# A later exponential in an attention pipeline, and a split, earlier load of the local q and k

## The chip, the cores and the metric

The kernel runs on one core of one Trainium2 chip. The metric is the device time of one execution in microseconds (us); of several runs the median is taken. The core has a matrix engine (TensorE, "PE" in the profile, with its weight loads as "PEld"), a vector engine (VectorE, DVE), an activation engine (ScalarE, ACT), a general engine (GpSimd, POOL) and an engine that issues transfers (SyncE, SP); each works through its own instructions in order, and semaphores tie them together. Sixteen DMA engines carry the transfers.

## The reference

Attention over 2 batches, 8 heads, 576 tokens and 64 features, in float32. Heads 0 to 3 see a local band (the 32 last positions), heads 4 to 7 a strided pattern (positions equal modulo 32, not later). The result, as 1152 tokens of 512 features, goes through two feed-forward stages.

```python
scores = scale * np.matmul(q, k.transpose(0, 1, 3, 2))
mask_local = (rel >= 0) & (rel < 32)
mask_strided = (rel >= 0) & (pos[None, :] % 32 == pos[:, None] % 32)
attn = softmax(np.where(masks, scores, -1e9)); x = attn @ v
for e in range(4): out += p[:, e:e+1] * (np.maximum(x @ w1[e], 0) @ w2[e])   # x 512 -> 1024 -> 512
gate = 1 / (1 + np.exp(-(out @ w_gate))); val = out @ w_val                  # 512 -> 1536
result = (gate * val) @ w_out
```

## The kernel before

**Attention as a pipeline written out by hand.** The work is cut into 32 groups, 16 for each batch: first 8 strided ones (kind "s"), then 8 local ones (kind "l"). A group passes six stages: `scores` (TensorE, two groups at once, lines 477 to 495, after a matmul that writes the mask into the PSUM tile `sps`), `exp` (VectorE takes the negated row maxima `nm`, line 503; ScalarE does four or three exponentials with their sums, line 505), `norm` (VectorE adds and inverts the sums, lines 512 and 513; GpSimd multiplies, line 514), `transpose` (TensorE, line 521; VectorE copies to the tile `PT`, line 524), `values` (TensorE, line 542; ScalarE copies, line 546; only where the second head of a pair has come) and `split` (VectorE writes the high part of x and GpSimd the low part, lines 561 to 568). The table `STAGES` says how many steps behind the scores a stage runs. In step i the generator `attention()` issues, in the order of the table, each stage for the group that is that many steps back; then a step may issue two matmuls without use (`keep_warm`, line 167), and the transposes that prepare q and k: `qk_strided` (lines 445 to 451) in steps 10 and 11 for the first pair of strided heads of batch 1 and 17 and 18 for its second, `qk_local` (lines 467 to 475) in steps 4 to 6 for batch 0 and 20 to 22 for batch 1. The tiles `sps`, `P`, `nm`, `sm` and `PT` have four buffers each.

**What runs around it.** `attend()` advances the generator by one step, and after some steps it issues loads on SP's queue: after step 6 the strided q and k of batch 1 (into `x2acc`), after step 8 strided values, after 11 the local q and k of batch 1, after 18 and 19 the token weights, after 20 local values. The first `FIRST_GROUPS` steps run alone; from step 14 on each is followed by one step of weight preparation (`prep_some`: a cast on ScalarE, line 425, or a subtraction on VectorE, line 427, in turn). The other 16 steps are interleaved with the matmuls of the first four units of the first feed-forward stage (0.36 steps for each three matmuls of lines 611 to 613). The rest of the kernel is matmul work of the two feed-forward stages, with the preparation of weights (casts and splits into a high and a low part) beside it.

**The order of the first loads on SP's queue**: strided q and k of batch 0 (8 transfers), strided values `vs` for the first pair, local q and k (`ql`, `kl`: 4 transfers of 288 KB), `vs` for the second pair, local values `vl` (5), token weights `ptok`, two pieces of weights `raw`, the strided q and k of batch 1, a third `raw`.

Of the kernel before, what the change touches and what calls it, by code (L numbers as in the profile page):

```python
# [9 lines left out]
F32 = mybir.dt.float32  # L10
# [19 lines left out]
PB_BUFS = 5  # L30
WARM = 11

STAGES = (("values", 6), ("transpose", 4), ("scores", 0), ("exp", 0), ("norm", 2), ("split", 7))
FIRST_GROUPS = 23
ATT_RATE = 0.36


# [1 line left out]
def attn_moe_glu_kernel(ctx, tc, q, k, v, dp, w1, w2, wg, wv, wo, out):  # L39
    nc = tc.nc  # L40
    B, H, S, D = q.shape
# [12 lines left out]
    hp = ctx.enter_context(tc.tile_pool(name="hp", bufs=2))  # L54
# [32 lines left out]
    def load_strided_v(b, c):  # L87
        h0 = 4 + 2 * c
        t = atp.tile([NU, 2, 8 * D], F32, tag="vs", name="vs", bufs=2)
        nc.sync.dma_start(t, v[b, h0:h0 + 2].rearrange("h (u r) d -> u h (r d)", r=8))  # L90
        qkv["vs", b, c] = t

    def load_local(b):
        for nm, src in (("ql", q), ("kl", k)):
            t = hp.tile([128, 9, 2, D], F32, tag="hh" if nm == "ql" else "hl", name=nm)
            for j in range(2):
                nc.sync.dma_start(  # L97
                    t[:, :, j, :],
                    src[b, 2 * j:2 * j + 2].rearrange("h s d -> (h s) d").rearrange("(c p) d -> p c d", p=128),
                )  # L100
            qkv[nm, b] = t

    def load_vl(b):
        t = atp.tile([128, 4, 6, D], F32, tag="vl", name="vl")
# [66 lines left out]
    def make_constants():  # L171

        diff = const.tile([NU, NU], I32, tag="diff", name="diff")
        msf = const.tile([NU, NU], F32, tag="msf", name="msf")
        nc.gpsimd.iota(diff, pattern=[[-1, NU]], base=4 * NU, channel_multiplier=1)
        nc.vector.tensor_scalar(diff, diff, 3, None, ALU.bitwise_and)
        nc.vector.tensor_scalar(msf, diff, 0.0, MASKED, ALU.is_gt, ALU.mult)
        make_identity(nc, ident)
        nc.gpsimd.tensor_copy(identb, ident)
        nc.gpsimd.affine_select(  # L180
            out=mask_s, in_=msf, pattern=[[-1, NU]],
            compare_op=ALU.is_ge, fill=MASKED, base=0, channel_multiplier=1,
        )
        nc.gpsimd.memset(mask_l, 0.0)
        for i0, i1, lead in ((0, 1, 0), (1, 4, 32)):
            m = mask_l[:, i0:i1, :]
            for sign, base in ((1, lead), (-1, 31 - lead)):
                nc.gpsimd.affine_select(
                    out=m, in_=m, pattern=[[0, i1 - i0], [-sign, 128]], compare_op=ALU.is_ge,
                    fill=MASKED, base=base, channel_multiplier=sign,  # L190
                )
# [267 lines left out]
    def qk_local(b, part):  # L459
        for nm, dst in (("ql", QT), ("kl", KT)):  # L460
            src = qkv[nm, b]
            if part == 0:
                dst["l", b] = atp.tile([128, 9 * 128], F32, tag=nm + "T", name=nm + "T")
            t = dst["l", b]
            ps = gp.tile([128, 512], F32, tag="g", name="qkps")
            for i in range(3):
                nc.tensor.transpose(  # L467
                    ps[:, i * 128:(i + 1) * 128],
                    src[:, 3 * part + i].rearrange("p j d -> p (j d)"), ident,
                )  # L470
            dd = t[:, part * 384:(part + 1) * 384]
            if nm == "ql":
                nc.scalar.activation(dd, ps[:, :384], AF.Copy, scale=SCALE)
            else:
                nc.vector.tensor_copy(dd, ps[:, :384])
# [94 lines left out]
    def attention():  # L570

        gs = []
        for b in range(B):
            gs += [("s", b, c, half, hh) for c in range(2) for hh in range(2) for half in range(2)]
            gs += [("l", b, c, half, hh) for half in range(2) for hh in range(2) for c in range(2)]
        n = len(gs)
        stage = dict(values=group_values, transpose=group_transpose, scores=lambda g: i % 2 or pair_scores(gs[i:i + 2]),
                     exp=group_exp, norm=group_norm, split=group_split)
        qk_strided(0, 0, (0,))
        for i in range(n + STAGES[-1][1]):  # L580
            for name, behind in STAGES:
                if 0 <= i - behind < n:
                    stage[name](gs[i - behind])
            if i == 0:
                qk_strided(0, 0, (1,))
            if i < 5 or i % 2 and i < FIRST_GROUPS:
                keep_warm(2)
            for b in range(B):
                at = i - b * n // B
                if b and at in (-6, -5):  # L590
                    qk_strided(b, 0, (at + 6,))
                if at in (1, 2):
                    qk_strided(b, 1, (at - 1,))
                if at in (4, 5, 6):
                    qk_local(b, at - 4)
            yield i


# [213 lines left out]
    with tc.manual_schedule():  # L812
        acc["x2"] = accp.tile([128, KC, NTOK], F32, tag="acc", name="x2acc")
        load_strided_qk(0, 0)
        load_strided_qk(0, 1)
        warm_up()
        make_constants()
        load_strided_v(0, 0)
        load_local(0)
        load_strided_v(0, 1)  # L820
        load_vl(0)
        nc.sync.dma_start(ptok, dp.rearrange("(t p) e -> p t e", p=128))
        load_raw_to(2)
        for T in range(NT - 1):
            alloc_x(T)

        def attend():

            i = next(att, None)
            if i == 6:  # L830
                load_strided_qk(1, 0)
                load_raw_to(3)
            if i == 8:
                load_strided_v(1, 0)
            if i == 11:
                load_local(1)
            if i == 13:
                load_strided_v(1, 1)
            if i == 18:
                token_weights()  # L840
            if i == 19:
                spread_token_weights()
            if i == 20:
                load_vl(1)
            return i

        att = attention()
        for i in range(FIRST_GROUPS):
            attend()
            if i >= 14:  # L850
                prep_some(0, 1)
        n_none = 0
        halves = x_half()
        for n, u in enumerate(units):
            if u == ("u", EARLY, 0):
                for _ in halves:
                    pass
            if u[0] == "u" and u[1] == NST:
                while u[2] not in x2_done:
                    split_x2(1)  # L860
            if n == N_EARLY:
                while attend() is not None:
                    pass
                at_stack.close()
                tmp["p"] = ctx.enter_context(tc.tile_pool(name="tmp", bufs=2, side="right", reuse_waits="tile"))
                alloc_scales()
                late.append(raw_next[0])
                tmp["g"] = ctx.enter_context(
                    tc.tile_pool(name="gp2", bufs=8 - PSUM_BUFS, space=PSUM, side="right", reuse_waits="tile"))
                tmp["w"] = ctx.enter_context(tc.tile_pool(name="wp2", bufs=W_BUFS_2, side="right", reuse_waits="tile"))  # L870
            while any(i in pieces_of(u) for i in waiting()):
                prep_some(n, 1)
            if u == ("d", NST, 0):
                acc["out"] = accp.tile([128, NTB, DM], F32, tag="acc", name="outacc")
            if n >= N_EARLY:
                load_p_some(n)
                load_p_some(n)
            for y in unit_steps(u):
                if n < N_EARLY and y is None:
                    n_none += ATT_RATE  # L880
                    while n_none >= 1:
                        attend()
                        n_none -= 1
                if y == "evac":
                    if n >= N_EARLY:

                        if gated:
                            split_x2(2)
                            continue
                        if x16_next[0] < 2 or n > units.index(("u", EARLY - 1, x16_next[0] - 1)):  # L890
                            if next(halves, "end") != "end":
                                prep_some(n, 1)
                                continue
                    prep_some(n, 3 if u[1] >= NST else 2)
            if u[0] == "d" and u[1] == NST - 1:
                gated.append(x2_half(u[2]))
# [28 lines left out]
```

## Time and profile before

| | |
|---|---|
| median of 3 runs | 683.96 us (681.36 to 684.11) |
| the profiled execution | 678.96 us, its span 677.2 us |
| TensorE busy in the span | 659.5 us, 97% |
| first matmul of the feed-forward work | 58.44 us into the span |
| TensorE's mean granted clock over the span | 0.992 of full |

The span runs from the first to the last instruction that the profiler saw on the core; the 1.76 us beside it lie outside. A busy TensorE is not one at its peak, since the ends of pipelined matmuls are modelled.

### The profile page before, as it was taken

What the parts mean: (1) busy time and instruction counts of PE and PEld (TensorE: products, weight loads), DVE (VectorE), ACT (ScalarE), POOL (GpSimd) and SP (SyncE); (2) the same over time, 40 slices, a digit from 0 to 9 for tenths busy, and PEclk for the clock granted to TensorE, in tenths of its full rate; (3) what the DMA queues carried; (4) which work ended last, traced back from release to release, by engine and by line L of the source; (5) the groups of instructions that cost most, each with busy time, mean ns of one, the idle gap of its engine ahead of it and who ended that gap; (6) DMA issues with size and microseconds to landing.
All of it is one profiled execution on the core that took longest, in us unless ns stands there. A gap on an engine that the chain in (4) does not pass through costs nothing.

```text
span 677.2 us, 11031 instructions
## 1 busy us (share of the span) xinstructions
PE 659.5 (97%) x4257; PEld 431.3 (64%) x4263; DVE 488.9 (72%) x986; ACT 268.9 (40%) x665; POOL 197.9 (29%) x218
## 2 busy tenths in 40 slices
PE   7879999999899999999999999999999999999998
PEld 4657899999766666666665656556655555555554
DVE  3685675878777787779798989887788998822212
ACT  5676541323334444442334252534354364331120
POOL 3463550000222222222354352522154244231110
PEclk9898999999999999999999999999999999999999
DMA  9953133011321233323222213111012321000002
GB/s 190 219 115 92 64 95 121 0 64 32 104 75 63 72 100 102 75 67 121 63 75 63 71 55 94 34 38 55 31 62 83 106 72 53 1 1 0 32 17 94
DMA packets 38965, 48.59 MB, mean 72 GB/s; under 512 B 18460, under 2 KB 23360, under 8 KB 38912
## 3 DMA queue, kind: packets, MB, share of 16 engines
q1 hardware_dynamic: 38912, 47.89, 24.8%
q8 instruction: 33, 0.54, 0.3%
q14 instruction: 20, 0.16, 0.1%
HBM read 45.50 MB, written 2.38 MB: 71 GB/s over the span
## 4 chain that ended last, share of the span: by engine, by line
PE 87%; DVE 8%; DMA 1%; issue 1%; ACT 1%; SPq 1%; POOL 0%; DVEq 0%; ACTq 0%; POOLq 0%
PE gps L611 27%; PE gps L612 27%; PE gps L613 27%; PE o L542 2%; PE sps L495 1%; PE tps L521 1%; DMA kl<-in_k_dram 1%; DVE x2acc L675 1%; DVE wpk L339 1%; SPq L97 1%; PE qkps L467 1%; DMA x2acc<-in_k_dram 1%; DVE x L290 1%; PE sps L485 1%; DVE magn L372 1%
## 5 line engine op out<-in xcount | busy, mean ns | idle before, releaser
L634 POOL TENSOR_TENSOR hl<-t,hh 128x384 f16<-128x384 f32 x72 | 69.3, 962 | 253.9 <-ACT t L633 249.9
L611 PEld LDWEIGHTS <-w 128*128 128x128 f16 x864 | 84.4, 98 | 56.2 <-issue 0.3
L613 PEld LDWEIGHTS <-w 128*128 128x128 f16 x864 | 84.4, 98 | 56.0
L612 PEld LDWEIGHTS <-w 128*128 128x128 f16 x864 | 84.4, 98 | 55.2
L632 ACT ACTIVATE hh<-gps 128x384 f16<-128x384 f32 x72 | 35.2, 489 | 148.2 <-PE gps L613 148.2
L612 PE MATMUL gps<-hl,w 128*128 128x384 f16 x288 | 94.0, 326 | 0.0
L611 PE MATMUL gps<-x,w 128*128 128x384 f16 x288 | 94.0, 326 | 0.0
L611 PE MATMUL gps<-hh,w 128*128 128x384 f16 x288 | 94.0, 326 | 0.0
L612 PE MATMUL gps<-x2p,w 128*128 128x384 f16 x288 | 94.0, 326 | 0.0
L612 PE MATMUL gps<-x,w 128*128 128x384 f16 x288 | 94.0, 326 | 0.0
L613 PE MATMUL gps<-hh,w 128*128 128x384 f16 x288 | 94.0, 326 | 0.0
L613 PE MATMUL gps<-x2p,w 128*128 128x384 f16 x288 | 94.0, 326 | 0.0
L613 PE MATMUL gps<-x,w 128*128 128x384 f16 x288 | 94.0, 326 | 0.0
L611 PE MATMUL gps<-x2p,w 128*128 128x384 f16 x288 | 94.0, 326 | 0.0
L698 POOL TENSOR_TENSOR hl<-gv,hh 128x384 f16<-128x384 f32 x36 | 34.7, 965 | 146.4 <-ACT hh L697 146.4
L355 DVE SCALAR_TENSOR_TENSOR w<-raw,up,w 128x512 f16<-128x512 f32 x48 | 38.3, 799 | 20.3 <-ACT w L353 20.3
L675 DVE TENSOR_TENSOR x2acc<-x2acc,t 128x384 f32<-128x384 f32 x84 | 49.6, 591 | 2.9
L672 DVE SCALAR_TENSOR_TENSOR t<-gps,comb,pb 128x384 f32<-128x384 f32 x72 | 43.8, 609 | 9.9 <-PE gps L613 9.9
L697 ACT CAST hh<-gv 128x384 f16<-128x384 f32 x36 | 18.4, 511 | 81.0 <-DVE gv L696 81.0
L696 DVE SCALAR_TENSOR_TENSOR gv<-gps,sg 128x384 f32<-128x384 f32 x36 | 19.9, 554 | 40.3 <-PE gps L613 40.3
L407 POOL TENSOR_TENSOR w<-magn,w 128x512 f16<-128x512 f32 x36 | 46.1, 1287 | 8.5 <-ACT magn L406 8.1
L505 ACT ACTIVATE P<-sps,nm 72x72 f32<-72x72 f32 (+1 forms) x112 | 36.3, 331 | 28.8 <-DVE sm L512 22.8
(130 smaller groups left out, 1236.2 us busy)
## 6 DMA issues: line engine op xcount, KB each, us to landing
raw<-in_moe_w_dram SPq DMA_DIRECT2D x32, 512.0 KB
raw<-in_moe_w_gate_dram SPq DMA_DIRECT2D x12, 512.0 KB
raw<-in_moe_w_val_dram SPq DMA_DIRECT2D x12, 512.0 KB
raw<-in_moe_w_out_dram SPq DMA_DIRECT2D x12, 512.0 KB
pb<-pd SPq DMA_DIRECT2D x11, 192.0 KB
out_dram<-outacc SPq DMA_DIRECT2D x8, 256.0 KB
vl<-in_v_dram SPq DMA_DIRECT2D x8, 160.0 KB
vs<-in_v_dram SPq DMA_DIRECT2D x4, 288.0 KB
```

The source lines that it names most:

```text
L355: nc.vector.scalar_tensor_tensor(wl[i][:, c, :], part, sc, wh[i][:, c, :], ALU.mult, ALU.subtract)
L407: nc.gpsimd.tensor_tensor(wl[i][:, c, :], f, wh[i][:, c, :], ALU.subtract)
L505: nc.scalar.activation(pp[:, j, :], pv_[:, j, :], AF.Exp, bias=nm[:n, j:j + 1], accum_out=sm[:n, j:j + 1])
L611: nc.tensor.matmul(ps, ah, bh, start=i == 0, stop=False)
L612: nc.tensor.matmul(ps, ah, bl, start=False, stop=False)
L613: nc.tensor.matmul(ps, al, bh, start=False, stop=i == n - 1)
L632: nc.scalar.activation(dh, ps, AF.Relu, scale=DOWN)
L634: nc.gpsimd.tensor_tensor(dl, t, dh, ALU.subtract)
L672: nc.vector.scalar_tensor_tensor(t, ps, cc, pb[e, T], ALU.mult, ALU.mult)
L675: nc.vector.tensor_tensor(a, a, t, ALU.add)
L696: nc.vector.scalar_tensor_tensor(gv, pv_, DOWN, sg, ALU.mult, ALU.mult)
L698: nc.gpsimd.tensor_tensor(dl, gv, dh, ALU.subtract)
```

## The change

The stages `exp` and all behind it run one step later against the scores, and the steps that run alone are 24, not 23, so that the number of steps interleaved with matmuls stays 16. `qk_local` runs in steps 5 to 7 and 21 to 23. The local q and k of batch 0 are loaded ahead of the first strided values, and in two parts: for the first three of nine columns of 128 rows, then for the other six. The steps at which `attend()` issues its other loads, and those of `qk_strided`, are the same numbers as before.

```diff
-STAGES = (("values", 6), ("transpose", 4), ("scores", 0), ("exp", 0), ("norm", 2), ("split", 7))
-FIRST_GROUPS = 23
+STAGES = (("values", 7), ("transpose", 5), ("scores", 0), ("exp", 1), ("norm", 3), ("split", 8))
+FIRST_GROUPS = 24
...
     def load_local(b):
-        for nm, src in (("ql", q), ("kl", k)):
-            t = hp.tile([128, 9, 2, D], F32, tag="hh" if nm == "ql" else "hl", name=nm)
-            for j in range(2):
-                nc.sync.dma_start(
-                    t[:, :, j, :],
-                    src[b, 2 * j:2 * j + 2].rearrange("h s d -> (h s) d").rearrange("(c p) d -> p c d", p=128),
-                )
-            qkv[nm, b] = t
+        for nm in ("ql", "kl"):
+            qkv[nm, b] = hp.tile([128, 9, 2, D], F32, tag="hh" if nm == "ql" else "hl", name=nm)
+        parts = [(0, 3), (3, 9)] if b == 0 else [(0, 9)]
+        for c0, c1 in parts:
+            for nm, src in (("ql", q), ("kl", k)):
+                for j in range(2):
+                    rows = src[b, 2 * j:2 * j + 2].rearrange("h s d -> (h s) d").rearrange("(c p) d -> p c d", p=128)
+                    nc.sync.dma_start(qkv[nm, b][:, c0:c1, j, :], rows[:, c0:c1])
...
-                if at in (4, 5, 6):
-                    qk_local(b, at - 4)
+                if at in (5, 6, 7):
+                    qk_local(b, at - 5)
...
         make_constants()
+        load_local(0)
         load_strided_v(0, 0)
-        load_local(0)
         load_strided_v(0, 1)
```

## Rows read from the trace of the kernel before

**Rows 1.** The page's head and its chain that ended last, by engine.

```profile
span 677.2 us, 11031 instructions
...
PE 87%; DVE 8%; DMA 1%; issue 1%; ACT 1%; SPq 1%; POOL 0%; DVEq 0%; ACTq 0%; POOLq 0%
```

**Rows 2.** Busy time by stage: length, engines' busy us (instructions), granted clock, DMA share, GB/s.

```profile
31.65:58.44 26.79, 23.03 (x260) 16.95 (x261) 20.44 (x65) 18.72 (x93) 14.55 (x20) 0.87 0.56 120
58.44:100.00 41.56, 40.16 (x349) 34.45 (x349) 28.99 (x84) 23.93 (x92) 21.18 (x28) 1.00 0.28 82
100.00:677.00 577.00, 570.80 (x3397) 362.65 (x3395) 423.53 (x785) 207.91 (x388) 150.89 (x145) 1.00 0.20 61
```

**Rows 3.** TensorE's timeline at the places used: start, length, instruction, idle before.

```profile
16.19 0.52 PE L467 MATMUL qkps<-ident,kl 128*128 128x128 f32 x3 [2.55 <-DMA kl<-in_k_dram]
...
27.60 0.49 PE L485 MATMUL sps<-ml,identb 96*96 96x384 bf16 x2
28.02 0.90 PE L495 MATMUL sps<-klT,qlT 64*96 64x128 f32 x12
28.85 0.72 PE L445 MATMUL qkps<-ident,x2acc 72*128 72x72 f32 x8
29.40 0.41 PE L521 MATMUL tps<-ident,P 72*72 72x72 f32 x4
30.62 0.59 PE L167 MATMUL warm<-const-float32-0.0 128*128 128x512 bf16 x2 [0.80 <-DVE ksT L451]
...
31.65 0.72 PE L542 MATMUL o<-PT,vs 72*64 72x72 f32 x16
...
58.44 0.44 PE L611 MATMUL gps<-xh,wh 128*128 128x384 f32 x1
```

**Rows 4.** The same windows view as rows 2, in short stretches of the first 56 us.

```profile
0.00:14.00 14.00, 12.09 (x113) 7.29 (x114) 5.54 (x18) 8.22 (x42) 4.99 (x17) 1.00 0.87 187
...
18.00:20.00 2.00, 2.00 (x12) 1.80 (x11) 0.59 (x4) 1.68 (x9) 0.66 (x1) 0.50 0.89 151
0.00:26.00 26.00, 20.96 (x211) 14.13 (x213) 11.10 (x35) 14.19 (x73) 7.33 (x20) 0.93 0.95 204
26.00:28.00 2.00, 1.65 (x19) 0.86 (x14) 1.74 (x9) 1.76 (x9) 0.67 (x2) 1.00 0.81 203
50.00:52.00 2.00, 2.00 (x22) 1.47 (x20) 1.11 (x3) 0.59 (x4) 0.00 (x0) 0.50 0.04 9
```

**Rows 5.** SP's queue in its timeline, and the chain's entry for kl (last line).

```profile
20.84 0.34 SPq L82 DMA_DIRECT2D x2acc<-in_k_dram  x1
...
10.17 5.89 DMA kl<-in_k_dram
```

**Rows 6.** VectorE's waits from 31.65 to 58.44 us: total, times, longest.

```profile
DVE nm L503 <- PE sps L495: 2.4, 3, 1.0
DVE PT L524 <- PE tps L521: 2.1, 4, 1.0
...
DVE ptokT L204 <- PE o L542: 0.7, 1, 0.7
```

**Rows 7.** ScalarE's and VectorE's timeline around the first exponentials.

```profile
6.59 0.45 DVE L503 TENSOR_REDUCE nm<-sps 72x4 f32<-72x288 f32 x1 [0.89 <-PE sps L495]
7.08 0.32 ACT L505 ACTIVATE P<-sps,nm 72x72 f32<-72x72 f32 x1 [1.68 <-DVE nm L503]
7.28 0.46 DVE L451 COPY ksT<-qkps 128x288 f32<-128x288 f32 x1 [0.23 <-PE qkps L445]
...
8.28 0.41 ACT L449 ACTIVATE qsT<-qkps 128x288 f32<-128x288 f32 x1
```

**Rows 8.** Groups by line up to 58.44 us: count, busy us, mean ns, idle before.

```profile
L427 DVE TENSOR_TENSOR wl<-raw,wh 128x512 fp32r<-128x512 f32 x4 | 3.6, 895 | 0.0
...
L473 ACT ACTIVATE qlT<-qkps 128x384 f32<-128x384 f32 x5 | 2.4, 481 | 0.0
```

**Rows 9.** TensorE's two longest waits from 58.44 to 100 us: total, times, longest.

```profile
PE gps L611 <- DVE hl L637: 0.8, 1, 0.8
PE gps L612 <- POOL xl L568: 0.6, 1, 0.6
```

## The prediction

> **What bounds the kernel now.** I began with the page's head and its chain. The chain lies on TensorE for 87% [rows 1], so the question is where TensorE does not work or works slowly. The windows by stage answer it: from 100 us to the end it is busy 570.8 of 577 us, and from 58.44 to 100 us 40.2 of 41.6, at full clock in both [rows 2]. Nothing in the change touches what is computed there. What can move is the head, the steps that run alone before the first feed-forward matmul at 58.44 us [rows 3]; whatever that matmul gains or loses, the busy 97 to 99% behind it carry to the end almost one to one.
>
> In the head I read TensorE's timeline for its waits and then the short windows for the clock. One wait stands out: 2.55 us for `kl`, until 16.19 us [rows 3]. Some 2 us later, at 18 to 20 us, the granted clock is 0.50, the lower of its two levels (1.2 GHz) [rows 4]. A second stretch at 0.50 lies around 50 us [rows 4]. From 31.65 us to the end of the head no engine is full: of 26.8 us VectorE works 20.4, ScalarE 18.7, TensorE 23.0 at a mean clock of 0.87 [rows 2]. The waits between the engines cost there, and VectorE's longest is for scores: three waits of 2.4 us together, before the maxima [rows 6]. That is the wait which the table of stages takes away.
>
> **The change part by part.** All terms are against the profiled execution, 678.96 us (span 677.2 and 1.76 outside); it is 5.0 us below the median of the runs, 683.96, to which I apply the sum at the end.
>
> *The loads, and where their gain stops.* The local q and k no longer have 288 KB of values ahead of them, and their first third needs 384 KB, not 1152. The 2.55 us therefore go, and ScalarE paces steps 1 to 9. The first maximum now stands behind a copy of k on VectorE, and starts at 7.74 (7.28 + 0.46), not 6.59; the first exponential follows 0.49 us later (7.08 against 6.59), at 8.2 us. Four exponentials take 1.2 us (7.08 to 8.28 [rows 7]). Eight groups of 1.2, two copies of q of 0.41 [rows 7] and three local ones of 0.48 [rows 8] make 11.9 us, so the eighth group is done at 20.1. The scores of step 10 need the buffers that it leaves; a pair of scores takes 1.25 us with its masks (27.60 to 28.85 [rows 3]), so TensorE has step 10's stages behind it at about 22 us, against 28.85 before: some 6.5 us of lead.
>
> But step 10 ends with the transposes of the strided q and k of batch 1, and these are still issued behind the same bytes as before. By the transfers' sizes, 2592 KB lie up to and with the last `kl` (strided 1152, values 288, local 1152). By 14 us 187 GB/s x 14 us = 2.62 MB had moved [rows 4]; the 2.65 MB are through at 14.2 us, and `kl` was there at 16.06 (10.17 + 5.89 [rows 5]), 1.9 us after its bytes. Up to the k of batch 1 come 288 KB of values, 768 of local values, 18 of token weights, 1024 of weights and 576 of itself and q: 5266 KB or 5.39 MB. By 26 us 204 x 26 = 5.30 MB had moved, and the rest at 203 GB/s [rows 4] is through at 26.4; with the same 1.9 us k arrives at **28.3 us**. The DMA engines are busy nearly throughout (0.95 of the 26 us [rows 4]), the order behind the local parts stays, so an earlier TensorE can't pull this in. Before, TensorE took it at 28.85 without a wait [rows 3]: it was just there. So TensorE waits again, from about 22 to 28.3 us, and of 6.5 us of lead **0.5 us** is kept. Bounds: 0, if it arrives at 28.85, and 2.5, if the 1.9 us were nothing.
>
> *One group behind at that point.* At the end of step 10 before, the transposes of group 6 had been issued; now those of group 5. From 28.85 to 31.65 us [rows 3] TensorE had two sets of q and k, one group's transposes and two warming matmuls before the values of group 6. Now there are, beyond these, another group's transposes (0.41) and a pair of scores (1.25), less the q set already done (half of 0.72), and less the 0.80 for which a warming matmul waited there on VectorE [rows 3], whose copies are now done by then: 0.4 + 1.25 - 0.35 - 0.8 = **+0.5 us** (0.4 to 1.3, with and without the 0.8).
>
> *The clock at that point.* A wait of 2.55 us was followed by half speed [rows 3, 4]; one of six us should be too. The path from k's arrival to the values of group 6 is 2.8 + 0.5 us, nearly all TensorE's. All of it at half speed would add 3.3, none if the clock is back; part of the slow stretch passes while TensorE still waits, and this wait is more than twice the first, so that more of the stretch should pass in it: I take **+0.9** (0 to 3.3).
>
> *The scores' wait.* From there the groups run as before, with the scores a step ahead. Those 2.4 us go: **-2.4 us**. The lower bound is 0: an exponential also waits until the `P` buffer of four groups earlier has been transposed, in the same step as ever, and VectorE's 2.1 us for transposes [rows 6] may take up what is freed. The upper is all three rows, 5.2 us.
>
> *One more step alone.* It adds one step of weight preparation. Ten of them are five subtractions instead of four, 0.90 us each [rows 8], on the engine that is nearest to full: **+0.7** (0 to 0.9). It also adds two warming matmuls, in TensorE's gaps: 0. Each `attend` load goes out one step earlier against the groups. SP's wait for the values of group 3, and later of groups 7 and 15, is thus one step longer; what is queued behind them (strided q and k for step 17, local ones for step 21, weights) has some ten steps of cover: 0, and a step's 2 us if it had not.
>
> *A fifth `PT` tile.* The token weights borrow a `PT` buffer after step 19. Before, the copy into it waited 0.7 us for group 14's values, the next thing on TensorE [rows 6]. Now a buffer is free for it, but group 15's copy in step 20 finds none until those values, which come only in step 21, after a pair of scores: VectorE stands some 2.0 us (1.25 and the values' 0.72) instead of 0.7, with the next maxima queued behind. Of the 1.3 I take **+0.6** (0 to 1.3), since ScalarE still has a group's work then.
>
> *Behind the head.* TensorE's waits of 0.8 and 0.6 us [rows 9] may shrink, since VectorE no longer stands for scores: **-0.3** (0 to -1.4).
>
> Sum: -0.5 + 0.5 + 0.9 - 2.4 + 0.7 + 0.6 - 0.3 = **-0.5 us**: 678.5 for the profiled execution and 683.5 on the median, 0.1% down.
>
> **A rule against the split.** A load takes SP 0.34 us to issue [rows 5], and DMA work stayed dense, 0.87 busy over the first 14 us, with many loads under way [rows 4]: transfers overlap, so that four more of them cost the stream almost nothing. The Trainium skill (DMA: Bandwidth & Descriptors, Bandwidth and Anatomy of one DMA) advises batches of 1 MiB or more and gives each transfer some 2.0 us of fixed time. By that rule, were it paid in turn, four more transfers would cost 8 us, and the sum would be +7; by the rows it is 0.
>
> **The rivals.**
> *The second slow stretch does not come.* The 0.50 around 50 us follows a passage in which TensorE waits for VectorE's token weights. If it is as long as the mean of 0.87 over 26.8 us says [rows 2], 26.8 x 0.13 / 0.5 = 7.0 us, half of it, 3.4 us at most, is lost there. If VectorE, rid of its waits, keeps TensorE busier there, 683.5 - 3.4 = 680.1. Against it: VectorE's work in that passage is the same or more.
> *The strided data is there in time.* If k is there when TensorE comes, at 22 us, the other 6.0 us of lead are kept and the 0.9 for the clock is not paid: 676.6. Against it stands the count of bytes: 5.39 MB in 22 us would be 245 GB/s, where the first 26 us show 204 [rows 4].
> *Other waits take the place.* The maxima come early, but each exponential waits for its `P` buffer: +1.8 of the 2.4, 685.3.
> *Slower: the new wait at step 10 costs the clock for longer.* If the six idle us bring half speed for twice as long as the 2.55 did, TensorE, 23.0 busy of 26.8 us [rows 2], becomes the bound in steps 11 to 14: all 3.3 us of the path instead of 0.9, and 1.7 of the 2.4 not gained, as VectorE then waits for transposes: 683.5 + 2.4 + 1.7 = 687.6. It decides from the point where more than 4 us of TensorE's work behind the wait run at 1.2 GHz.
> *Slower: the small transfers are paid in turn*, 1.9 us each by `kl`'s lag: four times that is 7.6 us later at step 10, 691.1. Nothing in the rows speaks for it.
>
> **How the numbers follow.** A measurement of this kernel can hardly tell 0.5%, 3.4 us, from no change: its three runs spread over 2.75 us. My forecast has 0.40 and the buffers' rival 0.13, together no change 0.53; the clock's gain 0.22 and the early data 0.05, faster 0.27; the long slow stretch 0.17 and the transfers 0.03, slower 0.20. The likeliest time is 683.5 (its own range 681 to 686). The range of 8 in 10 leaves out the transfers, the early data and the far edge of the two clock rivals: 678.6 to 687.8.
>
> **What would show it.** In the profile after: no wait for `kl` in steps 5 to 7; TensorE idle up to about 28 us with the k of batch 1 as the releaser, in `qk_strided` of step 10, and a granted clock of 0.5 near it; no waits of `nm` for `sps`; the first feed-forward matmul within 2 us of 58.4. If it comes below 55, the wait at step 10 was less than I think or the clock stayed up; above 61, the clock or the extra step cost more.

## The result and the profile after

The change made the kernel slower: 685.05 us against 682.18, medians of twelve runs each, a ratio of 1.0054 (95% interval 1.0032 to 1.0076). By that ratio it is 3.7 us (2.2 to 5.2), and the two medians lie 2.9 us apart, where 0.5 us less had been forecast. The profiled execution of the changed kernel took 686.38 us; the one before that the prediction worked from, 678.96, was among the quicker of its kernel, so the two profiles differ by 7.4 us, about twice as much.

The page's head, and its chain by engine:

```profile
span 684.6 us, 11041 instructions
...
PE 85%; DVE 9%; ACT 2%; DMA 1%; issue 1%; POOL 0%; ACTq 0%; DVEq 0%; POOLq 0%
```

The span has grown by 7.4 us ([rows 1] has 677.2). To see where, I cut both traces at the same two matmuls: the first of line 611 and its 49th, with which the fourth unit of feed-forward work begins. TensorE's timeline of the changed kernel has them at 63.12 and 108.83 us; in the kernel before they stand at 58.44 [rows 3] and 101.40. The short fence has its line for the second, and the values of group 10, which are used further down.

```profile
22.91 0.90 PE L495 MATMUL sps<-klT,qlT 64*96 64x128 f32 x12
28.94 0.71 PE L445 MATMUL qkps<-ident,x2acc 72*128 72x72 f32 x4 [5.13 <-DMA x2acc<-in_q_dram]
30.67 0.71 PE L445 MATMUL qkps<-ident,x2acc 72*128 72x72 f32 x4 [1.01 <-DMA x2acc<-in_k_dram]
...
36.25 1.23 PE L542 MATMUL o<-PT,vs 72*64 72x72 f32 x16
...
45.99 0.72 PE L542 MATMUL o<-PT,vl 128*64 128x96 f32 x12
...
63.12 0.42 PE L611 MATMUL gps<-xh,wh 128*128 128x384 f32 x1
...
108.83 0.33 PE L611 MATMUL gps<-hh,wh 128*128 128x384 f32 x1
```

```profile
38.22 0.72 PE L542 MATMUL o<-PT,vl 128*64 128x96 f32 x12
...
101.40 0.34 PE L611 MATMUL gps<-hh,wh 128*128 128x384 f32 x1
```

So the head is 4.68 us longer (63.12 less 58.44), the interleaved stretch between the two matmuls 2.75 us longer (45.71 against 42.96), and the rest is the same: 575.78 us from the second matmul to the end in both. The three numbers are the whole 7.4.

**The head.** The wait for `kl` [rows 3] is gone, and TensorE is ready for the strided q and k of batch 1 at 23.8 us instead of 28.85 (about 22 had been foreseen). There it waits 5.13 us for q and 1.01 for k. Behind the wait the windows view (columns as in [rows 2]) shows this:

```profile
0.00:26.00 26.00, 21.80 (x231) 14.41 (x233) 12.98 (x43) 16.79 (x86) 9.69 (x24) 1.00 0.88 195
24.00:28.00 4.00, 0.00 (x0) 0.00 (x0) 0.21 (x2) 0.87 (x6) 1.70 (x3) 1.00 1.03 306
30.00:44.00 14.00, 13.11 (x93) 9.77 (x96) 6.50 (x23) 6.20 (x29) 5.26 (x8) 0.50 0.69 161
46.00:63.12 17.12, 13.05 (x170) 10.15 (x170) 15.23 (x50) 13.86 (x70) 9.92 (x15) 1.00 0.35 85
```

Four us without TensorE work are followed by a granted clock of 0.50 (1.2 GHz) from 28.1 to 45.1 us, 17.1 us at a stretch, while TensorE is busy 13.1 of 14. From there to the end of the head the clock is full, and the second slow stretch of the kernel before [rows 4] does not come. The first row says something else too: in this execution 195 GB/s had moved 5.07 MB by 26 us, where [rows 4] have 5.30.

**The interleaved stretch.** VectorE's waits, and TensorE's, over its first 42 us:

```profile
DVE wl L427 <- ACT wh L425: 9.9, 8, 1.7
DVE PT L524 <- PE tps L521: 2.0, 3, 0.9
...
PE gps L611 <- DVE x2acc L665: 1.0, 2, 0.7
PE tps L521 <- DVE x2acc L665: 1.0, 1, 1.0
PE gps L611 <- DVE hl L637: 0.8, 1, 0.8
PE gps L612 <- DVE hl L637: 0.4, 1, 0.4
```

In the kernel before TensorE waited only the two times of [rows 9]. New is that VectorE's subtraction of a weight piece waits for ScalarE's cast of the same piece, eight times, and that TensorE waits for VectorE's emptying of PSUM. One such place in the timeline:

```profile
87.25 0.61 ACT L425 CAST wh<-raw 128x512 fp32r<-128x512 f32 x1
87.89 1.12 DVE L427 TENSOR_TENSOR wl<-raw,wh 128x512 fp32r<-128x512 f32 x1 [1.17 <-ACT wh L425]
88.93 0.54 DVE L665 TENSOR_TENSOR x2acc<-gps,x2acc 128x384 f32<-128x384 f32 x1
...
89.53 0.44 PE L611 MATMUL gps<-hh,wh 128*128 128x384 f32 x1 [0.69 <-DVE x2acc L665]
```

ScalarE gets to the cast late, the subtraction waits 1.17 us for it at the head of VectorE's queue, the PSUM tile behind it is emptied late, and TensorE waits 0.69 us for that tile.

### The profile page after: what moved, and what is told of

Read it like the earlier page. It is cut to its first block, busy times and chain, and to the rows that moved or that the text cites. A ratio compares the mean times of both kernels' runs of the same rounds, so it can differ in the third digit from the quotient of the medians.

```text
span 684.6 us, 11041 instructions
## 1 busy us (share of the span) xinstructions
PE 662.2 (97%) x4259; PEld 433.7 (63%) x4265; DVE 490.4 (72%) x986; ACT 269.1 (39%) x665; POOL 194.9 (28%) x218
## 4 chain that ended last, share of the span: by engine, by line
PE 85%; DVE 9%; ACT 2%; DMA 1%; issue 1%; POOL 0%; ACTq 0%; DVEq 0%; POOLq 0%
PE gps L611 26%; PE gps L612 26%; PE gps L613 26%; ACT P L505 1%; DMA x2acc<-in_k_dram 1%; PE sps L495 1%; PE o L542 1%; PE warm L167 1%; PE tps L521 1%; DVE nm L503 1%; DVE x2acc L675 1%; DVE PT L524 1%; DVE wl L427 1%; DVE wpk L339 1%; PE qkps L445 1%
```

## The experiments

**What they were to tell apart.** Theory A: the loss has two sources that have nothing to do with each other, the wait for strided data with the slow clock behind it, and the *turn* of the weight preparation. The preparation gives, in turn, a cast (ScalarE) and the subtraction that needs it (VectorE), one step at a time in the head and two at a time afterwards. After nine steps in the head, each later call is a subtraction whose cast was issued a call ago, and then a cast; after ten, a cast and at once its own subtraction. The added step in the head makes ten of nine. Theory B: the added step and the later stages themselves cost the time.

All thirteen kernels. The head, the interleaved stretch and the time at half clock in the head are those of the one profiled execution (us); the granted clock is the mean over a kernel's runs:

| kernel | median us | ratio to before | head | interleaved | half clock in the head | granted clock |
|---|---|---|---|---|---|---|
| before | 680.2 to 682.2 | 1 | 58.44 | 42.96 | 10.2 | 0.9887 |
| the change | 685.05 | 1.0054 (1.0032 to 1.0076) | 63.12 | 45.71 | 17.1 | 0.9881 |
| 1: nine steps of preparation | 680.88 | 1.0017 (0.9993 to 1.0041) | 61.69 | 42.51 | 17.1 | 0.9867 |
| 2: loads alone | 683.61 | 1.0035 (1.0013 to 1.0057) | 61.52 | 42.97 | 17.1 | 0.9855 |
| 3: stages alone | 683.86 | 1.0032 (1.0011 to 1.0053) | 62.24 | 45.74 | 13.7 | 0.9898 |
| 4: warming in the wait | 685.07 | 1.0068 (1.0042 to 1.0094) | 63.00 | 45.74 | 13.7 | 0.9916 |
| 5: strided first | 680.31 | 0.9988 (0.9965 to 1.0010) | 57.10 | 45.71 | 10.2 | 0.9920 |
| 6: strided first, nine | 673.83 | 0.9885 (0.9854 to 0.9915) | 52.48 | 42.51 | 0 | 0.9960 |
| 7: the same, old stages | 675.46 | 0.9919 (0.9886 to 0.9952) | 53.68 | 42.97 | 3.4 | 0.9930 |
| 8: before with ten steps | 685.27 | 1.0041 (1.0016 to 1.0065) | 59.92 | 45.83 | 17.0 | 0.9870 |
| 9: as 6 with eleven steps | 674.09 | 0.9905 (0.9874 to 0.9935) | 52.99 | 42.34 | 0 | 0.9973 |
| 10: as 6, unsplit | 673.54 | 0.9906 (0.9869 to 0.9942) | 52.80 | 42.51 | 0 | 0.9962 |
| 11: before, strided first | 676.71 | 0.9940 (0.9911 to 0.9968) | 58.43 | 42.94 | 10.2 | 0.9955 |

What follows the second cut took 575.7 to 575.8 us in every one of them.

**1. Nine steps of preparation.**

```diff
-            if i >= 14:
+            if i >= 15:
                 prep_some(0, 1)
```

> The changed kernel with the weight preparation beginning after step 15 and not 14, so that nine steps of it run in the head as before, not ten. Theory A (the turn of cast and subtraction): each later call does two steps of preparation; with nine done before, a call does a subtraction and then a cast, and with ten a cast and then its own subtraction, which waits. Then the interleaved stretch, 44.3 us in the changed kernel, comes back to about 41.6, VectorE's waits of line 427 for line 425 there go from 11.0 us to under 2, and the run is 2 to 3 us below the changed kernel, about the kernel before plus 1. Theory B (the later stages themselves make the stretch longer, as x comes a step later): the stretch stays near 44 us and the run gains at most the 0.7 us of one subtraction.

The stretch fell to 42.51. The run came to the level of the kernel before: 4.2 us lower by the medians, some 2.5 us by the two ratios to that kernel, which ran quicker beside this experiment (680.2 us). The 44.3 and 41.6 us above end the stretch earlier, at 107.43 and 100 us; the table ends it at 108.83 and 101.40. VectorE's and TensorE's waits over the first 42 us of the stretch:

```profile
DVE hl L637 <- ACT hh L636: 7.6, 6, 1.5
DVE PT L524 <- PE tps L521: 4.5, 6, 1.9
...
PE gps L612 <- POOL xl L568: 0.5, 1, 0.5
```

No subtraction waits for its cast. VectorE still waits 12 us, as long in all as in the changed kernel, but TensorE no longer waits for VectorE's emptying of PSUM: it stands once, for 0.5 us.

**2 and 3. The loads alone, the stages alone.** The first puts the new `load_local` and its place into the kernel before, the second takes them out of the changed kernel.

> The kernel before with the new load order and the split alone; stages, steps and preparation as before. Theory A (the wait has only moved to the strided q and k of batch 1 in step 10, and the clock falls for longer after it): no wait for kl, a wait of 4 to 7 us in step 10 ending near 30 us, granted clock 0.5 from about 28 us on for over 6 us, first feed-forward matmul at 60 to 63 us, 2 to 4 us slower than before. Theory B (the stages cost the time and the loads do not): the first feed-forward matmul at 58.5 or earlier, time as before or better.

> The changed stages and steps with the old load order, unsplit. Theory A: the wait of about 2.5 us for kl is back, now in step 5, step 10 finds its data nearly there (wait under 1.5 us), and the head ends between 56 and 59 us; the ten steps of preparation still cost 2 to 3 us in the interleaved stretch, so in all 0 to 2 us over the kernel before. Theory B (the added step is what costs the head): the head ends above 60.5 us although the clock falls no longer than before, and the run is 4 us or more slower.

The loads alone make the kernel slower, as theory A had it: TensorE waits 4.0 us for q and 1.0 for k, up to 30.78 us, the clock is 0.5 from 27.7 us for 17.1 us, and the interleaved stretch is the old one. The stages alone were worse than theory A's head of 56 to 59 us: the wait for `kl` is 1.5 us, but there is a wait of 1.9 and 1.2 us in step 10 all the same, and the clock falls behind that one, at 29.8 us for 13.7. Neither theory had that right: the head ends at 62.24, above theory B's 60.5, but the clock fell for longer than before, which theory B had not. Their interleaved stretch, 45.74, is that of ten steps.

What the split costs the transfers these runs don't isolate. TensorE took k at 29.77 us with the four old loads (experiment 3), at 30.67 with the eight of the change. But in experiment 8, with the same four loads in the same order, it took k by 27.57 us, so that two kernels with equal loads lie 2.2 us apart. And experiment 1, with the eight loads, had moved 204 GB/s x 26 us = 5.30 MB by 26 us, as much as the kernel before; still TensorE took k only at 30.33.

**4. Warming matmuls in the wait.**

```diff
+            if i == 10:
+                keep_warm(26)
```

> The changed kernel with 26 matmuls without use on TensorE in step 10, ahead of the strided transposes: about 5.6 us at full clock, the length of the wait. The data comes no earlier. Theory A (the clock behind the wait costs more than the wait): the granted clock stays 1.00 through 28 to 45 us, and the head ends 2 to 4 us sooner than the changed kernel's 63.1, at 59 to 61; the run is 2 to 4 us below the changed kernel. Theory B (VectorE and the number of steps set the pace, the clock does not): the head ends within 1 us of 63.1 and the run is as the changed kernel.

TensorE's timeline:

```profile
24.04 5.86 PE L167 MATMUL warm<-const-float32-0.0 128*128 128x512 bf16 x26
29.73 0.42 PE L445 MATMUL qkps<-ident,x2acc 72*128 72x72 f32 x4
30.54 0.44 PE L445 MATMUL qkps<-ident,x2acc 72*128 72x72 f32 x4 [0.40 <-DMA x2acc<-in_k_dram]
...
33.60 0.72 PE L542 MATMUL o<-PT,vs 72*64 72x72 f32 x16
...
40.37 0.72 PE L542 MATMUL o<-PT,vl 128*64 128x96 f32 x12
...
45.14 1.23 PE L542 MATMUL o<-PT,vl 128*64 128x96 f32 x12 [1.81 <-ACT of L546]
```

This was a half miss. The clock stays full behind the wait, and the passage from the values of group 6 to those of group 10 takes 6.77 us (33.60 to 40.37), where the changed kernel took 9.74 at half clock (36.25 to 45.99): there the clock costs 3 us. But then it falls at 44.5 us, for 13.7 us, around a wait of 1.81 us for ScalarE, and the head ends at 63.00 as if nothing had been done. To keep the clock in one place gave the head nothing here.

**5 to 7. The strided data ahead of the weights.**

```diff
         load_vl(0)
-        nc.sync.dma_start(ptok, dp.rearrange("(t p) e -> p t e", p=128))
-        load_raw_to(2)
...
-            if i == 6:
+            if i == 1:
                 load_strided_qk(1, 0)
+                load_raw_to(2)
+            if i == 6:
+                nc.sync.dma_start(ptok, dp.rearrange("(t p) e -> p t e", p=128))
                 load_raw_to(3)
```

The first is the changed kernel with this, the second has nine steps of preparation as well, the third has the stages and steps of the kernel before, with the new order of all loads.

> The changed kernel with the strided q and k of batch 1 issued ahead of the first weights (after step 1, not 6) and the token weights after step 6. 1042 KB less lie ahead of k. Theory A (the data of step 10 makes the wait, and the wait the slow clock): k arrives at about 25 us, TensorE waits under 3 us there, the head ends 3 to 5 us sooner than the changed kernel's 63.1; the interleaved stretch stays at 45.7 (ten steps of preparation). In all 681 to 683. Theory C (the clock falls in the head for some other lull if it doesn't fall there, as behind the warming matmuls): the slow stretch comes later, about 45 us, and the head ends at 60 or later.

> The same with nine steps of preparation in the head. Theory A: as the strided-first kernel, with the interleaved stretch at 42.5 to 43, about 2.8 us below it: 677 to 680, below the kernel before. Theory C: a slow stretch of 10 us or more somewhere in the head still, 679 to 682, no better than the kernel before.

> Both new load orders (local first and split, strided q and k of batch 1 ahead of the weights) under the stages and steps of the kernel before. If the later stages are worth the 2.4 us of waits for scores that the prediction gave them, this is 2 us or more above the strided-first kernel with nine steps of preparation; if they are worth nothing, it is the same within 1 us or lower, as it has a step less.

Without the wait the head of the first kernel has back more than it had lost: 57.10 us, against 63.12 in the changed kernel and 58.44 before. TensorE now waits 0.76 us at most for this data. The first kernel still has one slow stretch, 10.2 us from 40.4 us, as theory C had it, and yet ends its head 6 us sooner than the changed kernel. In the profiled execution of the second the clock never falls in the head, though three of its six runs have a mean clock of 0.992 and not 1.0. TensorE's timeline and the windows of that execution:

```profile
24.78 0.44 PE L445 MATMUL qkps<-ident,x2acc 72*128 72x72 f32 x4 [0.76 <-DMA x2acc<-in_k_dram]
...
52.48 0.42 PE L611 MATMUL gps<-xh,wh 128*128 128x384 f32 x1
```

```profile
0.00:52.48 52.48, 43.92 (x516) 31.06 (x523) 36.45 (x119) 37.18 (x186) 25.58 (x46) 1.00 0.81 182
52.48:95.00 42.52, 41.80 (x360) 35.72 (x359) 30.02 (x85) 24.02 (x92) 21.72 (x28) 1.00 0.29 84
```

It is 1.15% faster than the kernel before and better than I expected (677 to 680): the head is 6 us shorter. The first, with ten steps, kept its 45.71 and is 6.5 us slower than the second by the medians, 3.2 of them in the stretch and most of the others in the clock of its runs (0.9920 against 0.9960). The third is 1.6 us slower than the second by the medians, with runs from 673.9 to 680.1 us that overlap with the second's, so this pair does not settle what the later stages are worth.

**8 and 9. The turn, by itself.** The kernel before with `i >= 13`, so ten steps; the second kernel of the last group with `i >= 13`, so eleven.

> The kernel before with one thing changed: weight preparation begins after step 13, so ten steps of it run in the head. Theory A (the turn of cast and subtraction): the interleaved stretch goes from 42.96 to 45.5 to 46 us, and the run is 2.5 to 3.5 us slower than before. Theory B (only together with the later stages does the stretch grow): the stretch stays within 0.5 us of 43, the run within 1 us.

> The changed kernel with the strided q and k of batch 1 ahead of the weights and eleven steps of preparation in the head (from step 13). Theory A (what counts is the turn: an odd number of steps in the head makes each later call a subtraction and then a cast): the interleaved stretch is 42 to 43 us, as with nine. Theory B (more preparation in the head is what lengthens the stretch behind it, ten being worse than nine): it is 45.7 us or more. The head is 0.5 to 1 us longer than with nine; in all 673 to 677 by A, 677 to 681 by B.

Ten steps in the kernel before make its stretch 45.83, VectorE waits 9.5 us in eight places for casts, and the run is 0.41% slower:

```profile
DVE wl L427 <- ACT wh L425: 9.5, 8, 1.7
```

Eleven make 42.34. It is the turn and not the number: 9 and 11 give 42.3 to 43.0 in eight kernels, 10 gives 45.7 to 45.8 in five, whatever the stages and loads.

Experiment 8 shows a second thing. It takes k without a wait for a transfer that the profile names, its longest wait for one is 0.6 us (for `kl`), and still its clock falls, at 30.0 us for 10.2 us and at 50.5 for 6.8:

```profile
27.57 0.44 PE L445 MATMUL qkps<-ident,x2acc 72*128 72x72 f32 x4 [0.52 <-DVE sm L512]
```

```profile
31.00:40.00 9.00, 8.78 (x58) 5.95 (x56) 4.33 (x17) 3.92 (x19) 2.98 (x5) 0.50 0.84 180
```

So a long slow stretch comes without a long wait for data too.

**10 and 11. The split, and the old kernel with the strided data first.**

> The strided-first kernel with nine steps of preparation, and the local q and k of batch 0 in four transfers, not eight (ahead of the values still). If the split is what delays the stream, k of batch 1 arrives about 1 us earlier; the first local transposes wait for the whole kl, about 1 to 3 us in step 5. I expect the head 0 to 2 us longer than with the split, 673 to 677.

> The kernel before with one thing changed: the strided q and k of batch 1 ahead of the first weights, and the token weights after step 6. Local q and k are loaded as before. The wait for kl of 2.5 us stays, and with it a slow stretch near 17 us; step 10 had its data in time before. If the strided loads' place is worth something only together with the early local loads, the run is within 2 us of the kernel before, 680 to 682; if it takes time off by itself, 676 to 679.

Unsplit, TensorE waits 1.1 us for `kl`, and the run is the same (673.54 against 673.83): if the split is worth anything here, these six runs don't show it. The last was a surprise. In its profile it is the kernel before to 0.01 us at the end of the head, with slow stretches of the same lengths; but its median is 0.6% lower. Its runs have a higher granted clock, 0.9955 in the mean. So the new order takes about half of experiment 6's 1.15% off by itself, without the change.

**Time against clock.** The time goes with the clock. Of the 73 runs of the kernel before that were made beside the experiments, those at a mean clock of 0.985 took 683.5 us (median of 14), at 0.987 681.9 (13), at 0.990 680.0 (12) and at 0.992 678.9 (20): 4.6 us for 0.007 of 680 us, or 9.5 us at half speed, so each us at half clock costs about 0.48. The three runs of experiment 11 at 0.992 took 678.9 us too (median): its gain lies in its higher clock, and why the clock is higher the runs don't show. At equal clock the changed kernel is slower by more than the medians' 2.9 us, 685.8 at 0.987 and 684.1 at 0.990, 3.9 and 4.1 us; the one with nine steps took 680.8 at 0.987 (10 runs), 1.1 us less than the kernel before there. Such a comparison leaves out what a change does through the clock itself.

## Why the prediction was wrong

**The step that failed** is "One more step alone", with "Behind the head". I priced the tenth step of preparation as one more subtraction (+0.7 us) and the stretch behind it as a small gain (-0.3). It cost 2.75 us there, and 2.87 in experiment 8 by itself (45.83 less 42.96), by changing which instruction of a pair comes first in each later call. I had read that casts and subtractions come in turn, and that later calls take two steps, and did not put the two together. That term alone is three quarters of the 3.7 us. The tenth step costs the head more than the 0.7 as well: 63.12 us against 61.69 without it (experiment 1), with 17.1 us at half clock in both profiles. With nine steps the run is no slower than before beyond the noise (1.0017, 0.9993 to 1.0041).

**Where the gain of the loads stops** was right in place: TensorE waited for the strided q and k of batch 1, named as the releaser, in step 10. The arrival was off. I had k at 28.3 us with the stream unchanged; TensorE got it at 30.67, 1.8 us later than before, so that nothing of the lead was kept. By the same count the bytes up to k were through at about 27.2 us (5.07 MB by 26 us, the rest at the 260 GB/s of the next two), 0.8 later than I had; and k was taken 3.4 us behind them, not 1.9. In experiment 1 the bytes were through at 26.4, as I had counted, and k was taken 3.9 us behind. So the 1.9 us, read from `kl`, is the larger part of the error; why the lag is longer here stays open. The price of the four added transfers, which I took as free, stays open too: with eight loads k was taken at 30.33 to 30.78 us (the changed kernel, experiments 1, 2 and 4), with four at 29.77 (3) and by 27.57 (8), at most 3.2 us apart. The Trainium skill (DMA: Bandwidth & Descriptors, Anatomy of one DMA) gives some 2.0 us of fixed time to a transfer that GpSimd issues. Carried over to these, which SP issues, and paid in turn, four would make 8 us by it, an estimate that these runs don't bear out. (With the sum of -0.5 it gives +7.5, where the prediction has +7.)

**The clock at that point** was mis-sized: +0.9, with the slow stretch largely passing in the wait. It lasted 17.1 us, and from k to the values of group 6 it took 5.6 us (30.67 to 36.25), not 3.3; from there to group 10's another 3 were lost. This is the rival "the new wait at step 10 costs the clock for longer", to which I gave 0.17; its mechanism held for the head: TensorE was busy 13.1 of 14 us at half clock. What the other clock rival forecast, that the second slow stretch does not come, came about as well, and some was made up: at group 10 the changed kernel was 7.8 us behind (45.99 against 38.22), at the end of the head 4.7. That VectorE keeps TensorE busier there, as that rival had it, isn't shown: TensorE was busy 13.1 of the last 17.1 us. So the head's clock cost moved more than it grew: the runs' mean clock is 0.9881 against 0.9887. The profiled executions of kernels 6, 9 and 10 have no slow stretch in the head once the data is in time, and those of 5 and 7 shorter ones, so the wait goes with the long one. It isn't the only thing that does: experiment 8 has 17.0 us at half clock without such a wait, and experiment 11 gains clock though the kernel before had its data in time. What makes the clock fall, and why a stretch lasts 3.4 us in one place and 17 in another, stays open.

**The scores' wait** did go: VectorE's waits from 31.65 to the end of the head have no row for `nm` any more [rows 6]. What that is worth is only partly settled. At equal loads and preparation the later stages were better by the medians, 2.7 us from 2 to 1 and 1.6 from 7 to 6. Set against each other, the twelve runs each of 1 and 2 differ by 2.0 us in the mean (1.1 to 2.9), so there is a gain in that pair. But the profiled heads of 1 and 2 end within 0.2 us of each other, and at the clock of 0.987 that both have their runs differ by 0.7 us; that the gain comes from the scores' wait, as the 2.4 us had it, is not shown. At full clock groups 6 to 10 took 6.57 us before (31.65 to 38.22) and 6.77 with the later stages (experiment 4), so nothing was gained in that passage.

**A fifth `PT` tile** was there, but small: one wait of 0.3 us for group 14's values, where I had 2.0 for it; and the 0.7 us for which the token weights had waited [rows 6] went, so the +0.6 came out below zero.

**Right** were the place where the local loads' gain ends, the wait that it turns into, and that what happens in the head carries to the end: the last 575.7 to 575.8 us did not move in any of thirteen kernels. Not tried: the four more transfers in the old order of loads, and a longer head at the same clock.

## What to carry to other kernels

When a change shifts a loop by one step, look for everything that counts steps by twos: a helper that issues a producer and its consumer in turn can change from "consumer of the last, then next producer" to "producer, then its own consumer", and the engine in order then waits each time. A transfer moved forward is worth what the next transfer in the queue lets it be worth, so follow the stream's bytes to the next use and move that one as well: the same change with the strided loads ahead of the weights and an odd number of preparation steps took 1.15% off instead of adding 0.5, and about half of that came from moving the strided loads alone (experiment 11). Where the granted clock differs from run to run, read it beside the time before a difference of half a per cent is put down to the work itself: compare runs at equal clock, and compare the mean clocks as well, since a change can act through the clock.

## What the runs showed of the chip that I had not expected

TensorE stayed at 1.2 GHz for 17.1 us behind a lull of some six us, although the profile has it busy 13.1 of 14 us from 30 to 44 us; behind the lull of 2.55 us in the kernel before it was back after 3.4 us. With 26 matmuls in the lull it stayed at 2.4 GHz there, and fell 14 us later. In experiment 8 it fell at 30.0 us for 10.2 us, with TensorE busy 4.8 of the 6 us before and no single wait over 0.6. And executions of one program differ by it: the kernel before ran from 674.7 us at a mean clock of 1.0 to 684.6 at 0.985.
